# Group norm, one core: the last store of each run split into four gated transfers of every fourth row

## The chip, the cores and the metric

The kernel runs on one core of one Trainium2 chip. The metric is the device time of the whole program in microseconds (us); for this kernel it is read as the median of several executions. One execution was also recorded by the hardware profiler, and the profile and the trace are of that one.

## The reference

```
xr  = x.reshape(B, G, C // G, H, W)          # B 128, C 1024, H 32, W 16, G 32 groups, bf16
mu  = xr.mean(axis=(2, 3, 4), keepdims=True)
var = ((xr - mu) ** 2).mean(axis=(2, 3, 4), keepdims=True)
xn  = (xr - mu) / jnp.sqrt(var + 1e-5)
out = xn.reshape(B, C, H, W) * g[None, :, None, None] + b[None, :, None, None]
```

The input x and the output are 134 MB each; g and b are 1024 numbers each. Every element is read once and written once.

## The kernel before, in words

The work is cut into NT = 32 tiles of 128 rows. A row is one group of one sample: 32 channels of 512 numbers, 16,384 bf16 numbers, 32 KB that lie together in memory. A tile is four samples, 4 MB, one row to each SBUF partition. Six tile buffers xt0 to xt5 (NBUF = 6) are used in turn; a tile is normalized in place and stored from the buffer into which it was loaded.

For each tile TensorE adds up the columns with 32 matmuls (line 142) that wait for the load (line 140), VectorE turns the result into the negative mean (line 161), ScalarE squares and adds up the tile in two halves (line 255) and takes the root (line 276), VectorE forms scale and offset (lines 174, 177, 184) and applies them with 32 instructions (line 194). The last of these raises `s_dve`.

All loads and stores of tiles are issued by SyncE (SP), on one queue, in an order written out by hand in `sync_program`. First come the loads of tiles 0 to 5. Then, for each tile i, SP waits until VectorE has finished it, and issues its store (line 120), which raises `st[j]` by 16 when it has landed. After stores 1, 4, 7, ... 25 it issues the loads of up to RUN = 3 more tiles (line 113): each waits until the store that empties its buffer has landed. Transfers therefore alternate: three stores, three loads, three stores. Stores 26 to 31 have no loads behind them. At the very end SP waits for all stores (line 295).

```
def load(i):
    j = i % NBUF
    if i >= NBUF:
        sync.wait_ge(st[j], 16 * (i // NBUF))
    sync.dma_start(out=xt[j][:], in_=x_v[i]).then_inc(ld[j], 16)
```

A transfer of 128 rows is worked off by 16 DMA engines, in 128 packets of 32 KB and 16 small packets, one per engine, that report that engine's share as landed; the semaphore has risen by 16 when all engines have reported.

Of the kernel before, what the change touches and what calls it, by code (L numbers as in the profile page):

```python
# [17 lines left out]
NBUF = 6  # L18
RUN = 3
# [5 lines left out]
def kernel(  # L25
# [8 lines left out]
    P = nc.NUM_PARTITIONS  # L34
# [6 lines left out]
    NT = B0 // NS  # L41
# [8 lines left out]
    o_v = out.rearrange("(t n) (g k) h w -> t (n g) (k h w)", n=NS, g=G)  # L50
# [6 lines left out]
    xt = [sb.tile([P, F], BF16, name=f"xt{j}") for j in range(NBUF)]  # L57
# [19 lines left out]
    def sem(name):  # L77
        return tc.alloc_semaphore(name)

    ld = [sem(f"ld{j}") for j in range(NBUF)]  # L80
    st = [sem(f"st{j}") for j in range(NBUF)]
    s_gb, s_set, s_eye, s_rep = sem("s_gb"), sem("s_set"), sem("s_eye"), sem("s_rep")
    s_pe, s_mean, s_sq, s_std = sem("s_pe"), sem("s_mean"), sem("s_sq"), sem("s_std")
    s_dd, s_dve = sem("s_dd"), sem("s_dve")
# [23 lines left out]
    def sync_program(sync):  # L108
# [3 lines that stand above are left out]
                sync.wait_ge(st[j], 16 * (i // NBUF))  # L112
            sync.dma_start(out=xt[j][:], in_=x_v[i]).then_inc(ld[j], 16)

        for i in range(min(NBUF, NT)):
            load(i)
        for i in range(NT):
            j = i % NBUF
            sync.wait_ge(s_dve, i + 1)
            sync.dma_start(out=o_v[i], in_=xt[j][:]).then_inc(st[j], 16)  # L120
            if (NT - NBUF - 1 - i) % RUN == 0:
                for n in range(max(NBUF, i + 1 + NBUF - RUN), min(i + 1 + NBUF, NT)):
                    load(n)
# [162 lines left out]
    with tc.tile_critical():  # L286
        with nc.Block() as block:
            block.sync(sync_program)
            block.tensor(tensor_program)
            block.vector(vector_program)  # L290
            block.gpsimd(pool_program)
            block.scalar(scalar_program)

        for j in range(NBUF):
            nc.sync.wait_ge(st[j], 16 * len(range(j, NT, NBUF)))
# [30 lines left out]
```

## Time and profile before

| What | Value |
|---|---|
| median of 3 executions (lowest, highest) | 633.88 us (633.56, 633.88) |
| profiled execution: its own time | 632.89 us |
| profiled execution: its span | 631.1 us |
| busy share of the span | ScalarE 75%, VectorE 60%, TensorE 41% |
| DMA queue of the tiles: packets' time as a share of 16 engines | 99.0% |
| mean rate of the DMA engines | 425 GB/s |
| issue to landing, median | load 29.1 us, store 33.3 us |

The span is what the profile covers; the own time adds 1.8 us that lie around it. The three plain executions and the profiled one differ by up to 1.0 us. Each time in the trace counts from the start of the span.

### The profile page before, as it was taken

Reading aid. Unit: us, or ns where it says so; the run is one execution under the profiler, and the core shown is the slowest. Engines: PE = TensorE matmul, PEld = TensorE weight load, DVE = VectorE, ACT = ScalarE, POOL = GpSimd, SP = SyncE. Lnnn points to the kernel's source line nnn. Section 1 sums busy time; section 2 is a strip of 40 time slices with the busy share of each in tenths; the row PEclk is TensorE's granted clock in tenths of the full one; section 3 lists DMA queues with packets and bytes.
Section 4 is the critical chain, followed back from the end, with each engine's and each line's share of the span. In section 5 each row is a group of like instructions: output and inputs, shape, how many; then the busy total and the mean of one; then the engine's idle time right before and its main releaser. Section 6 shows DMA issues by size and latency. Waiting matters only on the chain. (4 is left out here: it accounts for less than half of the span.)

```text
span 631.1 us, 3670 instructions
## 1 busy us (share of the span) xinstructions
PE 260.1 (41%) x1025; PEld 106.2 (17%) x1025; DVE 375.6 (60%) x1188; ACT 476.2 (75%) x194; POOL 0.9 (0%) x7
## 2 busy tenths in 40 slices
PE   1877409008602750572087018604720670095000
PEld 0333103003201310230032003201310230032000
DVE  0067477774772777077627745770777177447771
ACT  0596999996994699199819965993899199749940
POOL 0000000000000000000000000000000000000000
PEclk9988858658855975687578659755975796588555
DMA  8999999999999999999999999999999999999996
GB/s 366 431 432 402 434 434 432 435 432 432 430 432 434 434 432 434 432 432 434 432 432 430 432 434 430 432 434 432 426 436 434 434 428 434 432 436 432 432 397 287
DMA packets 9320, 268.53 MB, mean 425 GB/s; under 512 B 1120, under 2 KB 1120, under 8 KB 1120
## 3 DMA queue, kind: packets, MB, share of 16 engines
q1 hardware_dynamic: 9216, 268.44, 99.0%
q14 instruction: 6, 0.05, 0.0%
q8 instruction: 2, 0.03, 0.0%
q10 hardware_dynamic: 96, 0.00, 0.0%
HBM read 134.22 MB, written 134.22 MB: 425 GB/s over the span
## 5 line engine op out<-in xcount | busy, mean ns | idle before, releaser
L255 ACT ACTIVATE ja<-xt,negmean 128x8192 fp8e5<-128x8192 bf16 x64 | 455.5, 7117 | 127.1 <-DVE jd L161 120.6
L142 PE MATMUL pa<-xt,eye 128*128 128x512 bf16 x1024 | 259.9, 419 | 309.1 <-PEq L140 306.9
L194 DVE TENSOR_SCALAR xt<-xt,scl,bia 128x512 bf16<-128x512 bf16 x1024 | 333.6, 405 | 1.2
L142 PEld LDWEIGHTS pa<-xt,eye 128*128 128x128 bf16 x1024 | 106.1, 106 | 462.5 <-issue 368.8
L161 DVE TENSOR_SCALAR_CACHE_REDUCE jd<-pa 128x512 bf16<-128x512 f32 x33 | 22.6, 685 | 144.6 <-PE pa L142 142.8
L174 DVE RECIPROCAL rstd<-std 128x1 f32<-128x1 f32 x32 | 5.2, 162 | 82.9 <-ACT std L276 82.9
L255 ACT ACTIVATION_READ_ACCUMULATOR ja<-xt,negmean 128x1 f32 x64 | 11.9, 186 | 0.0
L276 ACT ACTIVATE std<-sq,half 128x1 f32<-128x1 f32 x32 | 9.4, 294 | 1.0
L269 ACT ACTIVATE half<-sq,eps_t 128x1 f32<-128x1 f32 x32 | 8.9, 278 | 0.0
L184 DVE SCALAR_TENSOR_TENSOR bia<-scl,negmean,gb 128x32 f32<-128x32 f32 x32 | 8.0, 251 | 1.1
L177 DVE TENSOR_SCALAR scl<-gb,rstd 128x32 f32<-128x32 f32 x32 | 7.7, 242 | 1.1
L157 DVE COPY gb<-gb_p 128x64 f32<-128x64 f32 x1 | 0.2, 225 | 9.8 <-PE gb_p L128 9.8
L128 PE MATMUL gb_p<-gb_b,rep 32*128 32x64 bf16 x1 | 0.2, 231 | 10.8 <-DMA gb_b<-in_b_dram 10.8
L250 ACT ACT_TABLE_LOAD x1 | 1.3, 1283 | 1.9 <-issue 1.9
L161 DVE DVE_READ_ACCUMULATOR jd<-pa 128x1 f32 x33 | 2.7, 81 | 0.0
L128 PEld LDWEIGHTS gb_p<-gb_b,rep 32*128 32x128 bf16 x1 | 0.1, 100 | 10.8 <-DMA gb_b<-in_b_dram 10.8
L156 DVE MEMSET ones_b<- 128x128 bf16 x1 | 0.2, 165 | 1.1 <-SPq L286 1.1
L229 POOL TENSOR_SCALAR_AFFINE_SELECT rep<-ones_b 32x128 bf16<-32x128 bf16 x1 | 0.3, 305 | 0.0
L220 POOL TENSOR_SCALAR_AFFINE_SELECT eye<-ones_b 128x128 bf16<-128x128 bf16 x1 | 0.3, 294 | 0.8 <-DVE ones_b L156 0.8
L250 ACT ACTIVATE warm<-eps_t 128x1 f32<-128x1 f32 x1 | 0.2, 203 | 0.0
L238 POOL TENSOR_SCALAR eps_t<-ones_b 128x1 f32<-128x1 bf16 x1 | 0.2, 204 | 0.0
L310 POOL MEMSET const-bfloat16-1.0<- 128x1 bf16 x1 | 0.1, 102 | 0.0
(3 smaller groups left out, 0.3 us busy)
## 6 DMA issues: line engine op xcount, KB each, us to landing
xt<-in_x_dram SPq DMA_DIRECT2D x32, 4096.0 KB, 29.1
out_dram<-xt SPq DMA_DIRECT2D x32, 4096.0 KB, 33.3
gb_b<-in_g_dram ACTq DMA_DIRECT2D x1, 2.0 KB, 6.1
gb_b<-in_b_dram ACTq DMA_DIRECT2D x1, 2.0 KB, 9.3
```

The source lines that it names most:

```text
L128: pe.matmul(out=gb_p[:].rearrange("p a k -> p (a k)"), lhsT=rep[:], rhs=gb_b[:].rearrange("q a k -> q (a k)"), start=True, stop=True,).the ...
L142: m = pe.matmul(out=pa[j][:], lhsT=eye[:], rhs=xt[j][:, k * MM_FREE : (k + 1) * MM_FREE], start=(k == 0), stop=(k == NMM - 1),)
L161: dve.tensor_scalar(out=jd[i % 2][:], in0=pa[i % NBUF][:], scalar1=-inv_n, scalar2=None, op0=ALU.mult, op1=ALU.add, accum_out=col(negmean, i),
L174: dve.reciprocal(out=col(rstd, i), in_=col(std, i))._wait_ge(s_std, i + 1).then_inc(s_dd, 1)
L177: dve.tensor_scalar(out=scl[j][:], in0=gam, scalar1=col(rstd, i), scalar2=None, op0=ALU.mult,)._wait_ge(s_dd, 3 * i + 2).then_inc(s_dd, 1)
L184: dve.scalar_tensor_tensor(out=bia[j][:], in0=scl[j][:], scalar=col(negmean, i), in1=bet, op0=ALU.mult, op1=ALU.add,)._wait_ge(s_dd, 3 * i ...
L194: m = dve.tensor_scalar(out=span, in0=span, scalar1=scl[j][:, k : k + 1], scalar2=bia[j][:, k : k + 1], op0=ALU.mult, op1=ALU.add,)
L220: pool.affine_select(out=eye[:], in_=ones_b[:], pattern=[[-1, P]], compare_op=ALU.is_equal, fill=0.0, base=0, channel_multiplier=1,)._wait ...
L250: act.activation(out=warm[:], in_=eps_t[:], func=ACT.Sqrt)
L255: m = act.activation(out=ja[:], in_=xt[j][:, h * F // 2 : (h + 1) * F // 2], func=ACT.Square, bias=col(negmean, i), scale=1.0, accum_out=s ...
L269: act.activation(out=col(half, i), in_=sq[:, 2 * j : 2 * j + 1], func=ACT.Identity, bias=eps_t[:], scale=inv_n,)._wait_ge(s_sq, 3 * i + 1) ...
L276: act.activation(out=col(std, i), in_=sq[:, 2 * j + 1 : 2 * j + 2], func=ACT.Sqrt, bias=col(half, i), scale=inv_n,)._wait_ge(s_sq, 3 * i + ...
```

## The change

The stores behind which loads are issued, tiles 1, 4, 7, ... 25, nine of the 32, no longer go as one transfer. `gated` picks them out. `store_in_quarters` sends such a tile as four transfers c = 0 to 3, of rows c, c+4, c+8, ... (32 rows, 1 MB each). Transfers 0 and 1 are issued at once. Transfer 2 is issued when transfer 0 has landed on all DMA engines, transfer 3 when transfer 1 has landed. SP then waits until transfer 2 has landed, and goes on to the loads, which wait for `st[j]` as before; transfer 3 raises it. Nothing else is changed: the other 23 stores, the 32 loads and the programs of the other engines are the same.

```
+    qt = [sem(f"qt{c}") for c in range(3)]
...
+        def gated(i):
+            return i < NT - NBUF and (NT - NBUF - 1 - i) % RUN == 0
+
+        def store_in_quarters(i):
+            j = i % NBUF
+            n = 16 * (gates[0] + 1)
+            gates[0] += 1
+            for c in range(4):
+                if c >= 2:
+                    sync.wait_ge(qt[c - 2], n)
+                rows = slice(c, P, 4)
+                sync.dma_start(out=o_v[i][rows], in_=xt[j][rows]).then_inc(
+                    qt[c] if c < 3 else st[j], 16
+                )
+            sync.wait_ge(qt[2], n)
+
+        gates = [0]
...
-            sync.dma_start(out=o_v[i], in_=xt[j][:]).then_inc(st[j], 16)
+            if gated(i):
+                store_in_quarters(i)
+            else:
+                sync.dma_start(out=o_v[i], in_=xt[j][:]).then_inc(st[j], 16)
```

## The prediction

> **What bounds the kernel now.** I read the page's slices and its table of DMA queues first, then SP's waits and SP's timeline, then the chain of waits in order of time, and last the trace's packets and landings one by one.
>
> The page, slices and queue (tenths busy, GB/s; packets, MB, share of 16 engines):
>
> ```profile
> DMA  8999999999999999999999999999999999999996
> GB/s 366 431 432 402 434 434 432 435 432 432 430 432 434 434 432 434 432 432 434 432 432 430 432 434 430 432 434 432 426 436 434 434 428 434 432 436 432 432 397 287
> ...
> q1 hardware_dynamic: 9216, 268.44, 99.0%
> ```
>
> The DMA engines are full from the first slice to the last two. No compute engine passes 75%. So the time is the work of the DMA engines plus whatever the latest of the 16 loses.
>
> SP's waits (us in total, times, longest):
>
> ```profile
> SPq L120 <- DVE xt L194: 368.3, 23, 44.6
> SPq L113 <- DMA out_dram<-xt: 223.3, 25, 10.1
> ```
>
> SP waits nearly all the time, for computed tiles and for stores that have to land. It has room for more waits, as long as the engines keep work in their queue.
>
> One round in SP's timeline, three loads, then three stores:
>
> ```profile
> 464.19 19.70 SPq L113 DMA_DIRECT2D xt<-in_x_dram  x3
> 483.93 30.72 SPq L120 DMA_DIRECT2D out_dram<-xt  x3
> 522.75 19.66 SPq L113 DMA_DIRECT2D xt<-in_x_dram  x3
> ```
>
> Each load goes out when one more store has landed, 9.7 us apart; two stores are still queued when the first is issued.
>
> The chain in order of time, its second and last piece:
>
> ```profile
> 551.91 8.83 PE pa L142 x32
> ...
> 607.00 10.42 DVE xt L194 x32
> ```
>
> It begins when load 29 has landed (551.78 in the landings) and runs over three tiles of ScalarE work into store 31, issued at 617.44. Before 551.8 the DMA engines alone set the pace.
>
> Two stretches (the columns after the engines are clock, DMA share and GB/s):
>
> ```profile
> 230.00:270.00 40.00, 9.90 (x39) 4.13 (x40) 20.44 (x66) 26.51 (x13) 0.00 (x0) 0.62 1.00 433
> ...
> 613.00:618.00 5.00, 0.00 (x0) 0.00 (x0) 4.42 (x14) 0.00 (x0) 0.00 (x0) 0.50 0.37 157
> ```
>
> In mid-run nothing is idle. Between 613 and 618, while store 31's tile is being finished, eleven engines are already empty and five still work: they are late.
>
> **How late, and since when.** A packet of 32 KB takes 1.213 us and the next on its engine starts 3 ns before its end, so 512 packets an engine are 512 x 1.210 = 619.5 us. The first starts at 2.02 and the last ends at 628.87: the latest engine has lost about 7 us. Every transfer has 16 landings, and last minus first is the lag. It is 0.35 us at load 0, 1.5 at load 2, 2.3 at store 1 (81.5 to 83.7), 3.1 at store 3, 3.8 at load 16, 4.6 at load 22, 5.0 at load 25, 5.4 at load 28 and 5.5 to the end. Twelve, later eleven, engines stay within 1.0 us of each other. The step at store 3 is an instruction fetch (8 KB at 114.7, 0.31 us, beside a packet that is 0.46 late). The later ones, 0.7 + 0.7 + 0.4 + 0.4 = 2.2 us, all come at the end of a run of loads, when the late engines still read and the others already write: late reads there take 1.4 to 1.8 us instead of 1.213. The ends of the load runs at 103, 220 and 571 us show no such reads.
>
> **The change, part by part.**
>
> *Issues and completions.* 27 more transfers: 27 issues of 0.34 us on SP, which is idle there, and 3 more completions on each engine at nine places, 27 x about 6 ns = 0.2 us of engine time.
>
> *The hand-offs.* Behind each new wait stand, on SP, the next quarter, the loads, and then the next run's stores. A quarter is two packets an engine if 32 rows are spread like 128; the two gb_b loads of 32 rows each left 16 completions (96 packets = 2 x (32 + 16)), so 32 rows do use 16 engines. What covers each wait is the quarter still queued: 2 x 1.21 = 2.42 us on the latest engine. What has to fit under it: last packet's end to landing 0.33 us (628.87 to 629.20), landing to the next issue 0.02 (load 6 at 74.07 after store 0 at 74.06), issue to first packet 0.84 to 0.98 (store 31 at 617.44, first packets on idle engines at 618.28 to 618.42). Sum 1.2 to 1.35 us; 1.1 us to spare. So the latest engine never runs dry, at 3 x 9 = 27 hand-offs: cost 0. If the loop took 1 us more than its cover, it would be 27 us.
>
> *The loads.* Before, load i+4 was issued two stores early; now with one quarter queued. Its place in the queue is the same, and the loop above fits. The load of the gated tile's own buffer needs quarter 3, as it needed the whole store, at the same moment. SP reaches the next stores when it did.
>
> *What moves.* Engines that are ahead now run dry and wait: at the end of each run nobody leads the latest by more than the spare 1.1 to 1.2 us. The latest engine gets nothing back that it has lost. What can go is the later losses: with a lead of 1.2 us instead of 3 to 5, a late engine has at most one read left beside others' writes. Bounds: all 2.2 us go, or none (three load runs with lags of 2.3 to 5.5 us lost nothing, so lag alone doesn't decide). I take three quarters, 1.7 us, since the reads hurt are one to three per late engine and one could remain. A loss is also possible: see the second rival.
>
> The sum: 632.89 - 1.7 + 0.2 = 631.4 us for the profiled execution. The median lies 0.99 us higher; if that is lag it is cut too, if not it stays: 631.4 to 632.4, middle 631.9 us, -0.3%.
>
> *A rule against it.* The trace shows that a transfer queued behind others pays no start: tiles land 9.7 us apart and 8 x 1.21 is 9.68. The Trainium skill's page "DMA: Bandwidth & Descriptors", section Bandwidth, measures 6.15 us for 1 MB alone (78% of peak) against 97% at 16 MB. By that rate 36 quarters would be 36 x (6.15 - 2.42) = 134 us more, an estimate from that page; it counts a start that queued transfers here don't show.
>
> **The rivals.**
>
> *Slower, by shared paths.* No row shows which engine takes which row of a strided 32-row transfer. In 128-row transfers 16 engines run abreast at 1.213 us, so none is in another's way. If in the quarters two engines draw from the same part of SBUF, a packet takes up to the slowest seen, 2.51 us (at 58.75): 9 stores x 8 packets x 0 to 1.3 us = 0 to 94 us. Decisive from 0.05 us per packet on; I price it at half to whole, near 690 us. For it: rows of another shape. Against: quarters of every fourth row span all 128 partitions.
> The page "SBUF — State Buffer", section on the DMA port swizzle, has a port follow from the row number without its two lowest bits, and the first page gives engines groups of four rows; each engine would then keep its own port, and the cost would be 0. No run here shows it.
>
> *Slower, by engines in step.* Engines that were idle restart together, within 0.15 us. The only change from loads to stores made by engines in step, at 58 to 62 us (lag 0.35 on 15 of 16), stretched some 30 reads by 18 us in all, 1.1 an engine and up to 1.6. If that comes from being in step, eight further load runs would cost 8 x 1.1 to 1.6 = 9 to 13 us: 643 to 647 us. Against: no engine had begun to write then, and it was the first store of all. A small shortfall at the hand-offs, 27 x 0.2 to 0.4, would end at 639 to 645.
>
> *Nothing gained.* The late reads are lost whatever the lead: 633.9 plus 0.2, 633.2 to 634.8.
>
> That the quarters are not issued as told is excluded by the built program: SP's order has nine groups of four issues of 32x16384 and nothing else moved.
>
> **How the numbers follow.** Lag is cut: 0.48, 630.7 to 632.9. Nothing gained: 0.14. In step or short hand-offs: 0.18. Shared paths: 0.20. What a measurement here can tell is 0.2%, 1.3 us: 632.6 to 635.1 counts as the same. Faster 0.45 (nearly all of the first case), same 0.16, slower 0.39. The range leaves out shared paths: 630.5 to 650; the likeliest case alone has 630.7 to 632.9.
>
> **What would show it.** Right: landings of each transfer within about 1.5 us after the first gate, and no late reads over 1.5 us at the ends of load runs; packets of quarters at 1.213; the first packet of a load directly behind quarter 3 on the latest engine; the chain's start 1 to 2 us before 551.9. Wrong: packets of quarters over 1.3 us (shared paths); many reads of 1.5 to 2.5 us on all engines before each run of stores (in step); a DMA share below 1.00 on the latest engine around gates (hand-offs); a lag cut but the last landing where it was (nothing gained).

## The result, and the profile after

The changed kernel takes 649.76 us (median of 4 executions, 648.25 to 650.68) beside 633.88 us before: a ratio of 1.0249, 95% interval 1.0229 to 1.0269. It is slower by 15.9 us. The profiled execution took 648.25 us with a span of 646.5 us.

The page, slices, queue and the issues of the new transfers:

```profile
DMA  8999899999999999999999999999999999999998
GB/s 369 441 422 403 381 422 412 432 399 438 397 414 401 416 426 416 442 399 434 397 436 412 432 410 428 414 405 430 412 440 401 426 418 424 401 440 399 444 426 357
...
q1 hardware_dynamic: 9648, 268.44, 98.9%
...
out_dram<-xt SPq DMA_DIRECT2D x36, 1024.0 KB, 9.1
```

The DMA engines are as busy as before, 98.9%, but from the fifth slice to the last but one the rate swings between 381 and 444 GB/s; before, it stayed between 426 and 436 until the last two slices. They don't wait, they work more slowly in places. The queue has 27 x 16 = 432 more packets, as planned.

SP's waits:

```profile
SPq L129 <- DVE xt L217: 230.1, 9, 30.5
SPq L129 <- DMA out_dram<-xt: 181.4, 18, 21.0
SPq L143 <- DVE xt L217: 145.1, 14, 44.7
SPq L114 <- DMA out_dram<-xt: 31.0, 18, 2.1
```

The waits for stores have moved from the loads (223.3 us before) to the quarters; a load now waits for 2.1 us at most. SP's timeline, one round:

```profile
433.61 2.80 SPq L114 DMA_DIRECT2D xt<-in_x_dram  x3
436.45 1.84 SPq L143 DMA_DIRECT2D out_dram<-xt  x2
467.06 24.75 SPq L129 DMA_DIRECT2D out_dram<-xt  x4
493.81 2.79 SPq L114 DMA_DIRECT2D xt<-in_x_dram  x3
```

Three loads go out within 2.8 us instead of 19.7, and a round (load to load) has become 60.2 us long; it was 58.6. The chain, in order of time, is the same one, and begins 14.8 us later:

```profile
566.72 9.96 PE pa L165 x32
...
622.94 10.42 DVE xt L217 x32
```

Where the rate falls is seen in windows of the changed kernel, one at a change from stores to loads, one at a change from loads to stores, one amid stores (the last three columns are clock, DMA share, GB/s):

```profile
374.00:378.00 4.00, 0.00 (x0) 0.00 (x0) 3.34 (x11) 4.00 (x1) 0.00 (x0) 0.50 0.89 311
...
402.00:406.00 4.00, 1.23 (x6) 0.38 (x4) 4.00 (x14) 3.97 (x3) 0.00 (x0) 0.92 1.07 369
409.00:425.00 16.00, 7.44 (x27) 2.79 (x25) 11.73 (x39) 15.94 (x7) 0.00 (x0) 0.71 1.01 436
```

The kernel before, over the same two kinds of change:

```profile
361.00:366.00 5.00, 0.00 (x0) 0.00 (x0) 5.00 (x17) 4.97 (x3) 0.00 (x0) 0.50 0.97 419
388.00:396.00 8.00, 4.65 (x22) 1.91 (x20) 8.00 (x26) 7.97 (x3) 0.00 (x0) 0.94 1.02 434
```

For the experiments one number is used for each change of direction, called its excess: the time of the packets around it above 1.213 us, summed over all packets more than 30 ns late and divided by the 16 engines. It is worked out from the trace's single packets. Before, the nine changes from stores to loads cost 0.00 us each, and the ten from loads to stores 0.00 to 0.18, but for the first, 1.16. After, the nine cost 0.57 to 0.83, and the ten 0.85 to 1.15, but for the first, which comes ahead of any gate, 1.29. At a change to loads the slow packets are the first one or two reads (0.41 to 0.73 us of the excess) and the last writes ahead of them (0.05 to 0.40); at a change to stores they are the last one or two reads. Averaged over the 16 engines, all packets together took 17.6 us above 1.213 instead of 3.0, and an engine stood empty for 4.0 us instead of 2.8 between the first and the last packet: 14.6 + 1.2 = 15.8 us, which is the whole shift of the last packet's end (628.87 to 644.62).

### The profile page after: what moved, and what is told of

Same layout as the page of the kernel before. It is cut to its first block, busy times and chain, and to the rows that moved or that the text cites. A ratio compares the mean times of both kernels' runs of the same rounds, so it can differ in the third digit from the quotient of the medians.

```text
span 646.5 us, 3706 instructions
## 1 busy us (share of the span) xinstructions
PE 265.8 (41%) x1025; PEld 107.8 (17%) x1025; DVE 375.8 (58%) x1188; ACT 476.2 (74%) x194; POOL 0.9 (0%) x7
## 3 DMA queue, kind: packets, MB, share of 16 engines
q1 hardware_dynamic: 9648, 268.44, 98.9%
## 5 line engine op out<-in xcount | busy, mean ns | idle before, releaser
L165 PE MATMUL pa<-xt,eye 128*128 128x512 bf16 x1024 | 265.5, 425 | 318.7 <-PEq L163 316.4
L165 PEld LDWEIGHTS pa<-xt,eye 128*128 128x128 bf16 x1024 | 107.7, 107 | 476.1 <-issue 385.5
```

The source lines that it names most:

```text
L165: m = pe.matmul(out=pa[j][:], lhsT=eye[:], rhs=xt[j][:, k * MM_FREE : (k + 1) * MM_FREE], start=(k == 0), stop=(k == NMM - 1),)
```

## The experiments

Four theories are tested. A: engines that were brought together make each change at the same moment, and that slows reads. B: loads that are issued late start slowly. C: transfers of 32 rows disturb. D, formed when A fell: a queue that runs dry or nearly dry leaves the engines in a state that makes the next change to loads and the next change to stores cost 0.7 to 1 us each, whatever the lag.

**Quarters without waits** (e1_free).

```
+                if gated(i - NBUF):
+                    gates[0] += 1
+                    for c in range(3):
+                        sync.wait_ge(qt[c], 16 * gates[0])
...
-                if c >= 2:
-                    sync.wait_ge(qt[c - 2], n)
...
-            sync.wait_ge(qt[2], n)
```

> The four quarters are issued at once, without the waits between them; the loads go out as in the kernel before, each when all quarters of the store that empties its buffer have landed. Theory A (engines in step: the waits let engines that are ahead run dry, all restart together, and every change between stores and loads that 16 engines make together slows their reads): no waits, no step, so 633 to 635 us, excess of packet time per engine at the changes as before (1.9 us from loads to stores, 0 from stores to loads). Theory B (late loads: reads that are issued with less than one transfer of work queued ahead of them run slowly at first): loads are early again, so 633 to 635 us too. Theory C (the 32-row transfers themselves disturb the engines): 645 to 650 us as in the changed kernel.

Measured: 633.70 us, ratio 1.0003 (0.9993 to 1.0012), excess as before (0.00 at all changes to loads). C is out: 27 more transfers of every fourth row cost nothing that can be measured.

**The first store of a run gated, not the last** (e2_first).

```
-            ... (NT - NBUF - 1 - i) % RUN == 0
+            ... (NT - NBUF - 1 - i) % RUN == RUN - 1
```

> The first store of each run, not the last, goes in four gated quarters; the engines are still brought together once per run, but two whole stores (19 us of work) stand queued when the loads are issued. Theory A: the engines stay within some 1.2 us through the two stores, so both kinds of change cost what they cost in the changed kernel (about 0.9 us from loads to stores, 0.75 from stores to loads, per engine and change): 645 to 650 us. Theory B: reads that are issued early don't start slowly, so the 6.8 us from stores to loads go, 640 to 643 us.

Measured: 641.83 us, ratio 1.0136 (1.0111 to 1.0161). After the first gate the changes to loads still cost 0.49 to 0.88 us, with two whole stores queued when the loads were issued, and those to stores 0.65 to 1.04. The time lies where B put it, the excess where A put it. B as it stood is out: a change with loads issued early costs too. But there it isn't mainly the loads that start slowly: 0.41 to 0.64 us of each change lie in the last packets of the stores, which have the loads queued behind them, and 0.02 to 0.24 in the first reads.

**One gate only** (e3_once).

```
-            return i < NT - NBUF and (NT - NBUF - 1 - i) % RUN == 0
+            return i == 13
```

> One gated store only, tile 13; the others go whole as before. Theory A: the changes behind tile 13 are slow while the engines stay together, and the cost fades as they drift apart, about 0.75 us at the change right behind the gate and 0.9 at the next, perhaps a second pair at less: 634.5 to 637 us, with excess at changes that have no gate. Theory B: only the one change behind the gate costs, 0.75 us: 633.5 to 634.7 us, and the change from loads to stores after it costs nothing.

Measured: 635.57 us, ratio 1.0033 (1.0020 to 1.0046). The excess is 0.74 us at the change behind the gate and 0.91 at the next, which has no gate; then 0.00, 0.01, 0.00, 0.08. Two changes pay for one gate.

**Halves for quarters** (e4_halves).

```
-            for c in range(4):
-                if c >= 2:
-                    sync.wait_ge(qt[c - 2], n)
-                rows = slice(c, P, 4)
+            for c in range(2):
+                rows = slice(c, P, 2)
...
+            sync.wait_ge(qt[0], 16 * gates[0])
```

> Two halves of every second row in place of four quarters, both issued at once; the loads are issued when the first half has landed, with 4.84 us of the second half queued. An engine can then lead the latest by up to 4.84 - 1.25 = 3.6 us, where quarters leave 1.2. Theory A: the lag of the kernel before (2.3 to 3.8 us until load 16) is hardly touched, the engines stay apart: 632 to 636 us, excess at the changes near that of before. Theory B: the loads are issued with half a transfer queued, so first reads are slow on all engines at nine changes: 637 to 641 us.

Measured: 638.65 us, ratio 1.0095 (1.0056 to 1.0135), between the two. The lag stayed at 2.0 to 3.4 us, yet changes to loads cost up to 0.89 and changes to stores, after the first, 0.13 to 0.67. The cost of a change to loads follows how nearly the engines ran dry: where loads were issued at 128.73 and the early engines ended the second half at 129.9, it was 0.89; at 304.99 with the end at 307.3 it was 0.01. Over all nine it was 0.89 and 0.39 with 1.2 and 1.3 us left, and at most 0.23 with 1.8 us or more. A doesn't explain that. The changes to stores don't follow it: those at 101 and 512 us cost 0.62 and 0.60 though the changes to loads before them had cost 0.03 and 0.07, and no theory here covers that. The trace is of an execution of 636.93 us; the five range from 636.50 to 642.87.

**Stores issued after the reads have ended** (e5_latestore).

```
+            if 2 <= i <= 26 and (i - 2) % RUN == 0:
+                sync.wait_ge(s_ld, min(i + NBUF, NT))
...
+            pe.sem_inc(s_ld, 1)
```

The new semaphore `s_ld` counts the loads that TensorE has waited for.

> The changed kernel, but the first store of each run is issued only when the last load has landed on all engines, so that no write stands in any queue while the reads end. Theory A with its slow part made by the writes that follow: the last reads of a load run return to 1.213 us, the 0.9 us per change from loads to stores goes, and each such change pays 1.3 to 1.5 us of empty queues instead: 653 to 658 us. Theory A with its slow part in the ending of the reads themselves: the reads stay slow and the empty queues come on top, 661 to 665 us.

Measured: 656.12 us, ratio 1.0349 (1.0332 to 1.0365). From the second on, all changes from loads to stores have an excess of 0.00, while those to loads keep 0.74 to 0.90. Windows before and after the change at 103 us:

```profile
100.00:103.00 3.00, 3.00 (x16) 1.27 (x13) 0.25 (x2) 2.97 (x5) 0.00 (x0) 1.00 0.81 350
103.00:105.00 2.00, 1.18 (x7) 0.44 (x6) 1.93 (x7) 2.00 (x1) 0.00 (x0) 1.00 0.19 82
```

The queue is empty now, so the share falls to 0.19. So the last reads, slow in the changed kernel, aren't where no stores stand queued behind them. That doesn't make the kernel faster: engines stood empty for 18.9 us, 14.9 more than in the changed kernel, against 6.7 less of slow packets.

**Eight engines a step behind** (e6_stagger).

```
+            parts = [slice(0, P, 4), slice(1, P, 4), slice(2, P, 4)]
+            parts += [slice(3, P, 8), slice(7, P, 16), slice(15, P, 16)]
...
+                if c in (2, 3):
...
```

> The changed kernel with all its waits, but the fourth quarter goes as 16 rows on 16 engines and twice 8 rows, which the eight lowest engines alone take: eight engines leave each gate with three packets queued, eight with one, 2.4 us apart. Eight engines have 1.2 us more work per gate, 11 us in all. Theory A: the engines are apart at the changes, the excess falls from 0.75 to 0.9 us per change to under 0.4, about 9 of 16 us, and the time stays within 645 to 653 us. Theory B, or any in which the waits themselves cost the time: the excess stays, the work comes on top, 658 to 663 us.

Measured: 687.78 us, ratio 1.0847 (1.0830 to 1.0864); none of the expectations. The new pieces themselves were slow: of the 16 packets of the 16 rows, every eighth one, that began at 135.56 to 136.34, fourteen took 2.35 to 2.73 us, twice 1.213, and two 1.80 and 2.26. It tells nothing of A, but is what the first rival of the prediction, shared paths, describes, in another shape.

**Engines apart from the start** (e7_apart).

```
+            if i == 1:
+                parts = [slice(0, P, 2), slice(1, P, 4), slice(3, P, 8)]
+                parts += [slice(7, P, 16), slice(15, P, 16)]
...
```

> The kernel before, without any gate; only load 1 goes in five pieces (64, 32, 16, 8 and 8 rows), so that the eight lowest engines take nine packets and the others seven: the engines are 2.4 us apart from then on. Theory A: the first change from loads to stores, which all engines made together and which cost 1.0 to 1.2 us per engine, now costs under 0.4; the latest engine has 0 to 1.2 us more work: 632.5 to 634.5 us. If that first change was slow because the output is touched for the first time, it stays slow: 633.9 to 635.1 us.

Measured: 637.77 us, ratio 1.0060 (1.0045 to 1.0075). The first change to stores costs 0.07 us instead of 1.16, so a first touch of the output is not its cause. But the small pieces of load 1 were slow too; the 16 rows, again every eighth one, took 2.1 to 2.8 us a packet:

```profile
18.00:30.00 12.00, 4.51 (x21) 1.86 (x19) 0.70 (x2) 6.71 (x1) 0.00 (x0) 0.90 0.99 232
```

Twelve microseconds at 232 GB/s cost more than the 1.1 us that were saved, and they may have had a part in the 0.07; the run can't tell that from the engines' being apart.

**Loads issued after all stores have landed** (e8_lateload).

```
             sync.wait_ge(qt[2], n)
+            sync.wait_ge(st[j], 16 * (i // NBUF + 1))
```

> The changed kernel, but the loads of each run are issued only when the fourth quarter has landed too, so that no write is under way when the reads begin. Theory A with its cost in reads that meet writes still under way: the first reads of a load run return to 1.213 us, the 0.75 us per change from stores to loads goes, each such change pays 1.3 to 1.6 us of empty queues instead: 654 to 658 us. Theory A with its cost in 16 engines that begin to read at once: the first reads stay as slow as the first reads of the program (0.6 us per engine over 1.213), with the empty queues on top: 660 to 665 us.

Measured: 663.07 us, ratio 1.0461 (1.0444 to 1.0479). The first reads stay slow, 0.60 to 0.73 us, with no write under way: it is the start of reads by empty engines that costs, as at the program's start.

**A gate behind every second run** (e9_alternate).

```
-            ... (NT - NBUF - 1 - i) % RUN == 0
+            ... (NT - NBUF - 1 - i) % (2 * RUN) == 0
```

> The changed kernel with a gate behind every second run only: tiles 1, 7, 13, 19 and 25, five gates in place of nine. Theory A, with what one gate at tile 13 showed (0.74 us at its own change, 0.91 at the next, nothing at the change from stores to loads after that): 5 x 1.65 = 8 us over the kernel before, less what lag is cut: 640 to 643 us. If the cost of a gate built up over the runs behind it: 646 us or more.

Measured: 641.82 us, ratio 1.0118 (1.0101 to 1.0135), as the sum of single gates says. Here A falls. Windows at 83 us (gated) and 104, then 134 (no gate) and 162:

```profile
82.00:86.00 4.00, 0.00 (x0) 0.00 (x0) 2.71 (x9) 4.00 (x1) 0.00 (x0) 0.50 0.78 270
102.00:105.00 3.00, 1.76 (x9) 0.59 (x6) 2.25 (x8) 2.97 (x5) 0.00 (x0) 1.00 0.95 317
132.00:136.00 4.00, 0.00 (x0) 0.00 (x0) 3.52 (x12) 3.97 (x3) 0.00 (x0) 0.50 1.07 459
161.00:164.00 3.00, 0.17 (x1) 0.00 (x0) 3.00 (x10) 2.97 (x3) 0.00 (x0) 0.98 1.06 448
```

The rate is 270 and 317 GB/s in the first pair, 459 and 448 in the second (windows this short count whole packets by their start: at or over the 433 of mid-run means no loss, and low rates are rough, so the excess is the measure). The excess is 0.77 and 0.92, then 0.01 and 0.06, though the lag at the third change, 0.81 us, is as small as at the first, 0.75. At the ungated changes at 490 and 519 it is 0.5 and 0.9 us, with excesses of 0.00 and 0.07. Engines in step pay nothing if no gate came before. The first and the third change aren't quite alike, since 15 engines landed within 0.15 us at the first and within 0.57 at the third; the single stop below gives a closer pair.

**A whole store queued when the loads go out** (e10_second).

```
             if (NT - NBUF - 1 - i) % RUN == 0:
+                if i < NT - NBUF:
+                    sync.wait_ge(st[(i - 1) % NBUF], 16 * ((i - 1) // NBUF + 1))
```

> The kernel before, no quarters; the loads of each run wait until the last store but one has landed, so one whole store, 9.7 us of work, stands queued when they are issued, where the kernel before has two and the halves had 4.8 us. Theory D (dry queue: when the engines' queues run dry or within about a microsecond of it, the next change to loads and the next change to stores each cost 0.7 to 0.9 us on every engine, whatever the lag): 9.7 us less the lag and the 1.25 us of the hand-off leaves 3 us or more, no cost: 633 to 635 us. If every later issue of loads costs something: 636 us or more.

Measured: 633.49 us, ratio 0.9987 (0.9977 to 0.9996); all changes to loads at 0.00 to 0.03 us. Late loads as such are free, as long as the queue stays filled. The 0.13% is less than the prediction's bound of 0.2%.

**One full stop amid stores, whole transfers** (e11_stopstores).

```
             sync.wait_ge(s_dve, i + 1)
+            if i == 12:
+                sync.wait_ge(st[11 % NBUF], 16 * (11 // NBUF + 1))
```

> The kernel before with whole transfers only and a single full stop amid a run of stores: store 12 is issued when store 11 has landed on all engines. The loads behind are issued as early as before. Theory D: idle queues of 1.3 us and some of the lag, then 0.6 to 0.9 us at the change to loads behind tile 13 and 0.7 to 1.0 at the change to stores after it, nothing at later changes: 635.5 to 638.5 us. If pieces or late loads are needed for the cost: no excess at either change, 634.5 to 636.5 us.

Measured: 637.95 us, ratio 1.0060 (1.0043 to 1.0077). The stop is at 288.5 us. Windows at the four changes that follow it:

```profile
308.00:312.00 4.00, 0.00 (x0) 0.00 (x0) 1.75 (x6) 4.00 (x1) 0.00 (x0) 0.50 0.66 262
337.00:340.00 3.00, 0.05 (x1) 0.00 (x0) 3.00 (x10) 2.97 (x2) 0.00 (x0) 1.00 1.01 350
367.00:371.00 4.00, 0.00 (x0) 0.00 (x0) 3.87 (x12) 4.00 (x1) 0.00 (x0) 0.50 0.97 418
396.00:399.00 3.00, 0.38 (x2) 0.13 (x2) 3.00 (x10) 2.97 (x3) 0.00 (x0) 0.97 0.97 404
```

Rates of 262 and 350 GB/s, then 418 and 404; excesses of 0.90 and 0.70, then 0.01 and 0.09, with a lag of only 0.5 to 0.7 us at all four: at the two changes to stores, the same small lag goes with 0.70 and with 0.09. Of the 0.90, 0.72 us lie in the last packets of the stores, which began at 307.7, just ahead of the first window (so 262 is too low), with the loads queued behind them; 0.18 lie in the first reads. The first payment comes 20 us and two whole stores after the stop, at loads that had been issued as early as in the kernel before. No piece and no late load is needed.

**One full stop amid loads** (e12_stoploads).

```
+            if i == 18:
+                sync.wait_ge(s_ld, 18)
...
+            pe.sem_inc(s_ld, 1)
```

> The kernel before with whole transfers only and a single full stop amid a run of loads: load 18 is issued when load 17 has landed on all engines. Theory D, as at the program's start: the first reads of load 18 take about 0.6 us more per engine, the change to stores behind load 19 costs 0.7 to 1.0, the change to loads after that nothing: 636 to 638.5 us. If the cost belongs to a change of direction right behind the wait: only the stop itself, 635 to 636.5 us, and no excess at the next change to stores.

Measured: 638.95 us, ratio 1.0073 (1.0057 to 1.0090). The first reads after the stop (319 to 322), the change to stores (338 to 341) and the change to loads after that (368 to 372):

```profile
319.00:322.00 3.00, 3.00 (x9) 1.08 (x8) 0.00 (x0) 0.00 (x0) 0.00 (x0) 0.50 0.98 339
338.00:341.00 3.00, 3.00 (x15) 1.18 (x12) 1.76 (x6) 3.00 (x1) 0.00 (x0) 1.00 0.97 295
368.00:372.00 4.00, 0.00 (x0) 0.00 (x0) 1.76 (x6) 4.00 (x1) 0.00 (x0) 0.50 0.91 393
```

First reads are up to 1.0 us late, the change to stores costs 1.05 us, the next to loads 0.01. D holds in both places. It is the same picture as the program's start, where first reads were late and the first change to stores cost 1.16.

## Why the prediction was wrong

*The bound* was right: the DMA engines set the pace in both kernels, and the chain only starts later.

*The failed step is "The hand-offs".* The prediction set the cost of 27 hand-offs to 0, since the loop of 1.2 to 1.35 us fits under 2.42 us of queued work. The loop does fit: the latest engine moves on without a gap (quarters 0 to 3 of tile 13 land on it at 248.39, 250.82, 253.24 and 255.67 us), and engines stand empty only 1.2 us longer in all. What was missing is that a nearly empty queue has a price that is paid later, in slow packets: about 0.75 us at the change to loads and 0.9 at the change to stores. Nine gates x 1.65 = 14.9 us, where 14.6 us of slow packets were measured.

*"What moves"* was right in its mechanism and wrong in its worth. The lag was cut: 0.3 to 1.0 us at the end of the gated stores instead of 2.3 to 5.4. But nothing came of it: the 1.7 us of late reads that should have gone are about what a single gate costs.

*Shared paths* did not happen: quarters ran at 1.213 us a packet, the last ones right ahead of the loads aside, and the free quarters cost nothing. Packets of every eighth row took twice that time. That agrees with the port rule of the Trainium skill's page "SBUF — State Buffer", section on the DMA port swizzle, by which every fourth row reaches all 16 ports and every eighth only half of them; no run here shows the ports themselves.

*Engines in step* named the packets (reads of 1.5 to 2.5 us on all engines before each run of stores) and came nearest in price, 643 to 647 us. Being in step is not enough as a cause, as every second gate and the single stop show, and it left out the changes to loads, 6.8 us. The case that it was in was given 0.18.

*The rule against it*, 6.15 us for a transfer of 1 MB on the skill's page "DMA: Bandwidth & Descriptors", section Bandwidth, would by the prediction's estimate have made 134 us of it; measured are 15.9 us by 36 quarters, 0.44 us each, and 0 without waits. So even the sign of that rule came out here only with the waits.

*Open* is what the engines lose when they run dry. The runs show that it doesn't need pieces, late loads or a change of direction at the stop, that a small lag alone doesn't cost it, that it lasts over two whole stores, and that the pair of changes ends it. They also show where the time goes. With the other direction already queued, it goes mostly to the last packets before the change, reads or writes; with loads issued to empty engines, to the first reads (0.60 to 0.73 us when all stores had landed). Where in the engines it lies, no record here tells. Nor is it settled whether the engines must be close together as well: the first change cost only 0.07 us with them 2.9 to 4.7 us apart, but halves cost 0.89 at a lag of 3.3, twelve engines within 0.6.

## What to carry to other kernels

A queue of large transfers that alternates between loads and stores should not be let run near empty: in this kernel a wait that keeps only some 2.4 us of work queued looked covered and cost 1.65 us, half of it some 30 us later, while 9.7 us queued cost nothing. The lag of a DMA engine is time that it has already lost: no run here in which waits brought the engines together got any of it back. When a wait is costed, look at the packets of the next two changes of direction too, not only at the gap behind the wait.

## What the runs showed of the hardware that was not expected

- After a stop of the DMA queue, or when it was left with 2.4 us of work, the next change from stores to loads, or the next begin of reads, cost 0.5 to 0.9 us per engine, and the next change from loads to stores 0.65 to 1.15 us. In the runs with a single stop the later changes cost 0.0 to 0.1 us, but for one of 0.28.
- The last reads ahead of a store run were slow only when the stores already stood in the queue: 0.00 us of excess when they were issued after the reads, at some 1.7 us of empty queue each (14.9 us over nine). Last writes with loads queued behind them slow down likewise: 0.41 to 0.72 us where the loads had been issued 15 to 20 us before.
- Of a store of 16 rows, every eighth one, fourteen of 16 packets took 2.35 to 2.73 us; those of 32 rows, every fourth one, took 1.213.
